# A fused attention and two-MLP kernel on one core: values in pairs, loads spread over the steps, and the last groups' scaling on ScalarE

## The chip, the core and the metric

The kernel runs on one core of a Trainium2 chip, as one program. The metric is the device time of one execution in microseconds. Three executions of the kernel before took 1492.85, 1494.42 and 1499.25 us; their median is 1494.42 us.

## What is computed

Talking-heads attention over 4 batches, 12 heads, 448 positions and head size 64, followed by two MLPs. All operands are float32.

```python
scores = scale * np.matmul(q, k.transpose(0, 1, 3, 2))
scores = np.einsum('bhij,hg->bgij', scores, w_pre)
scores = scores - np.max(scores, axis=-1, keepdims=True)
attn = np.exp(scores)
attn = attn / (np.sum(attn, axis=-1, keepdims=True) + 1e-09)
attn = np.einsum('bhij,hg->bgij', attn, w_post)
return np.matmul(attn, v).astype(np.float32)
...
gate = 1.0 / (1.0 + np.exp(-(x @ w_gate)))
val = x @ w_val
return (gate * val @ w_out).astype(np.float32)
...
h = np.maximum(x @ w_in, 0.0)
return (h * h @ w_out).astype(np.float32)
```

## The kernel before

The program issues every instruction by hand in one order (`tc.manual_schedule`), and each engine runs its own share of that order strictly in sequence. So the order of the work is decided in Python, in the function `attention` and in the generator `mlp`, which `whole` advances a piece at a time whenever `attention` yields.

**Units.** A batch's 448 rows are cut into four row tiles (110, 110, 110 and 118 rows, the last padded to 120), and a tile into groups of 10 rows (`GI`); there are 180 groups (`NG`) in all. A group lies in memory with 10 rows times 12 heads on 120 partitions, so that mixing over heads is one matmul with a block matrix. Two tiles make a chunk (8 chunks).

**Functions, by line of the profile.** `scores(n, p)` (L176) computes two heads' q times k for a whole tile, copies the two results out of PSUM, one on ScalarE (L189) and one on VectorE (L187), into `e`, and stores them with DMAs (L198) into the group layout `g`. `split(s)` makes a rounded part `gh` on ScalarE (L212) and the rest `gl` on GpSimd (L213). `premix(s)` mixes the heads on TensorE into `ps_m` (L222; three matmuls, of which the trace shows two as `gh` and one as `gl`). `maximum(s)` is on VectorE (L230), `exponent(s)` on ScalarE with the row sums (L238), `normal(s)` on VectorE (add L244, reciprocal L247) and then on GpSimd, which scales the post-mixing matrix by the reciprocal sums into `wn` (L249). `postmix(s)` multiplies with `wn` (L264, eight matmul records), and `mixed` copies the result into the chunk's `ap` on VectorE (L276). `values(c, h)` multiplies a head pair's `ap` with v (L293, sixteen records); `valued` copies it on ScalarE (L308) and stores it to `xs` (L309). `k_load` is at L148, `q_load` at L156, `v_load` at L283; k has 10 buffers (`KB`) of which 6 (`NP`) serve a batch, v has 4, and a chunk needs six v loads.

**Steps.** The main loop takes one step `s` for each group: premix of group s, what is pending from the step before (copies of postmix and values, v loads), maximum of s, exponent of s-1, normal of s-2, split of s+2, and then further TensorE work until an estimate `left_over` of the step's time is used up: scores of a later tile if they are ready, and from the list `back` either postmixes of groups up to s-3 (`LAG`) or, once a chunk's postmixes are all issued, its six `values`. Values may not stand in the step of the chunk's last postmix. The estimates are those of L24:

```python
MW, PW, VW, SW, STEP = 0.62, 0.82, 1.66, 1.04, 2.41
```

So one values, or two postmixes, or one postmix and one scores fill a step. The scores of a tile are ready from two steps before the tile before it begins, all six at once; the k load that replaces a used k is issued with the scores that use it, and a v load in the step after the values that free its buffer.

**The MLP's share.** In the last 112 steps (`EARLY`) the loop also yields to `mlp`: one piece for every three steps that have passed, but only in a step in which no postmix was issued; after the last scores, one piece a step. The first 28 pieces load and split the first `x` (L582, L598, L599) and prepare the first weights, in the stages `w_load` (L473), `w_bias` (ScalarE, L483), `w_high` (VectorE, L489 and L492), `w_low` (VectorE, L505 and L512), `w_sum` (GpSimd, L523), `w_round` (ScalarE, L529) and `w_rest` (GpSimd, L537). The MLPs' matmuls are at L669; the first of them are issued between the values of the last chunk, if their operands' pieces have been issued by then.

Of the kernel before, what the change touches and what calls it, by code (L numbers as in the profile page):

```python
# [11 lines left out]
ALU = mybir.AluOpType  # L12
# [7 lines left out]
HV = 2  # L20
LAG = 3
LA = 5
NA = 9
MW, PW, VW, SW, STEP = 0.62, 0.82, 1.66, 1.04, 2.41  # L24
KB = 10
# [29 lines left out]
def attention(tc, q, k, v, w_pre, w_post, xs, B, H, S, D):  # L55
# [10 lines left out]
    nc = tc.nc  # L66
    JT = S // JP
    NP = H // 2
# [12 lines left out]
    NG = len(groups)  # L81
# [6 lines left out]
    with ExitStack() as ctx, ExitStack() as mid, ExitStack() as left:  # L88
# [18 lines left out]
        wq = one.tile([KM, H, GI], F32, name="wq")  # L107
# [42 lines left out]
        def q_load(n, p0=0, p1=NP):  # L150
            if p0 == 0:
                q_t[n] = p2.tile([P, NP, IM], F32, tag="q", name="q")
            n0, isz = sum(full[:n]) * H * D, full[n]
            n1 = n0 + isz * H * D
            x = q[n0:n1].rearrange("(d p i) -> d p i", d=P, p=NP)
            nc.sync.dma_start(out=q_t[n][:, p0:p1, :isz], in_=x[:, p0:p1])  # L156
# [4 lines left out]
        def scores(n, p):  # L161

            b, i0, rows = tiles[n]
            isz = full[n]
            if p == 0:
                g_t[n] = pg.tile([KM, GT, S], F32, tag="g", name="g")
            kt = k_t.pop((b, p)) if i0 + rows == S else k_t[b, p]
            ps = [
                ps_b.tile([P, S], F32, tag="b", name="ps_s")
                if n == 0 and p % 2  # L170
                else ps_q.tile([P, S], F32, tag="q", name="ps_s")
                for _ in range(2)
            ]
            for o in range(2):
                r = slice(o * D, (o + 1) * D)
                nc.tensor.matmul(  # L176
                    ps[o][:isz], lhsT=q_t[n][r, p, :isz], rhs=kt[r], start=True, stop=True
                )
            if n == 0 and p >= 3:
                e = [pa.tile([IM, S], F32, tag="a", name="e0") for _ in range(2)]  # L180
            else:
                t = p4.tile([IM, 2, S], F32, tag="e", name="e")
                e = [t[:, o] for o in range(2)]
            to = g_t[n].rearrange("(r h) g j -> h r g j", h=H)
            for o in range(2):
                if o:
                    nc.vector.tensor_copy(e[o][:isz], ps[o][:isz])  # L187
                else:
                    nc.scalar.copy(e[o][:isz], ps[o][:isz])  # L189
                e0 = 0  # L190
                for m, (g0, g1) in enumerate(blocks(b, i0, i0 + rows)):
                    e1 = e0 + (g1 - g0) * GI
                    move = (to[2 * p + o, :, g0:g1], e[o][e0:e1])
                    if m:
                        second.append(move)
                    else:
                        queue = nc.scalar if n == 0 and o and p in (1, 3, 4, 5) else nc.sync
                        queue.dma_start(out=move[0], in_=move[1])  # L198
                    e0 = e1
# [16 lines left out]
        def premix(s):  # L216
            n, r0, rows = groups[s][:3]
            kk = rows * H
            ps = ps_m.tile([P, S], F32, tag="m", name="ps_m")
            hi, lo = parts.pop(s)  # L220
            for m, (w, x) in enumerate(((0, hi), (1, hi), (0, lo))):
                nc.tensor.matmul(  # L222
                    ps[:kk], lhsT=wp[w][:kk, :kk], rhs=x, start=m == 0, stop=m == 2
                )
            a_t[s] = ps

        def maximum(s):
            kk, ps = groups[s][2] * H, a_t[s]
            nm = pa.tile([KM, 1], F32, tag="nm", name="nm")
            nc.vector.tensor_reduce(out=nm[:kk], in_=ps[:kk], op=ALU.max, axis=AX.X, negate=True)  # L230
            a_t[s] = [ps, nm]

        def exponent(s):
            kk = groups[s][2] * H
            ps, nm = a_t[s]
            a = pa.tile([P, S], F32, tag="a", name="a")
            sm = pa.tile([KM, 1], F32, tag="sm", name="sm")
            nc.scalar.activation(a[:kk], ps[:kk], AF.Exp, bias=nm[:kk], accum_out=sm[:kk])  # L238
            a_t[s] = [a, sm]

        def normal(s):
            kk = groups[s][2] * H
            sm = a_t[s][1]
            nc.vector.tensor_scalar(  # L244
                out=sm[:kk], in0=sm[:kk], scalar1=1e-9, scalar2=None, op0=ALU.add
            )
            nc.vector.reciprocal(out=sm[:kk], in_=sm[:kk])  # L247
            wn = pa.tile([KM, H, GI], F32, tag="wn", name="wn")
            nc.gpsimd.tensor_scalar(  # L249
                out=wn[:kk], in0=wq[:kk], scalar1=sm[:kk], scalar2=None, op0=ALU.mult  # L250
            )
            a_t[s] = [a_t[s][0], wn]

        ap, pending = {}, []
# [58 lines left out]
        starts = [next(s for s in range(NG) if groups[s][0] == n) for n in range(NT)] + [NG]  # L313

        k_order = iter([(b, p) for b in range(B) for p in range(NP)])
        v_order = iter([(c, hv) for c in range(len(chunks)) for hv in range(H // HV)])

        def load_next(load, order):
            x = next(order, None)
            if x is not None:  # L320
                load(*x)


        front = []
        for n in range(1, NT):
            front += [(max(starts[n - 1] - 2, 0), starts[n] - LA, n, p) for p in range(NP)]
        def due(s):

            return any(z - 1 - i <= s for i, (_, z, _, _) in enumerate(front[:NP]))

        back = []
        for c, ch in enumerate(chunks):
            back += [(postmix, PW, s) for s in range(ch[3], ch[4])]
            back += [(values, VW, c, h) for h in range(0, H, 2)]
        bpos, closed, posted, behind = 0, False, {}, 0

        def next_scores():
            _, _, n, h = front.pop(0)
            scores(n, h)
            if tiles[n][1] + tiles[n][2] == S:  # L340
                load_next(k_load, k_order)
            if h == 0 and n + 1 < NT:
                q_load(n + 1)

        def flush():
            now, pending[:] = list(pending), []
            for f, *x in now:
                f(*x)
# [14 lines left out]
        for s in range(NG + 30):  # L363
            if s < NG:
                premix(s)
            flush()
            if s < NG:
                maximum(s)
            if s in (4, 5, 6, 7):
                load_next(v_load, v_order)  # L370
            if 8 <= s < 8 + KB - NP:
                load_next(k_load, k_order)
            if 1 <= s <= NG:
                exponent(s - 1)
            if 2 <= s < NG + 2:
                normal(s - 2)
            if s + 2 < NG:
                split(s + 2)
            left_over = STEP - MW
            ready = front and front[0][0] <= s  # L380
            if ready and due(s):
                next_scores()
                ready, left_over = False, left_over - SW
            while bpos < len(back) and (left_over > 0.5 or s >= NG):
                f, cost, *x = back[bpos]
                if f is postmix:
                    if x[0] > s - LAG:
                        break
                    posted[groups[x[0]][3]] = s
                elif posted[x[0]] == s:  # L390
                    if s < NG:
                        break
                    flush()
                elif posted[x[0]] == s - 1 and ready:
                    next_scores()
                    ready = False
                if len(pending) > 3:
                    flush()
                f(*x)
                if f is values and (x[1] + 2) % HV == 0:  # L400
                    pending.append((load_next, v_load, v_order))
                bpos += 1
                left_over -= cost
                if f is postmix and x[0] == NG - 1:
                    flush()
                    mid.close()
                if s >= NG:
                    yield 3 if bpos == len(back) or back[bpos][0] is values else 2
            if ready and left_over > 0.4:
                next_scores()  # L410
            if not front and not closed:
                left.close()
                closed = True
            if NG - EARLY <= s < NG:
                behind += 1
                if closed:
                    yield 2
                elif behind >= 3 and s not in posted.values():
                    behind -= 3
                    yield 1  # L420
# [406 lines left out]
```

## Time and profile before

| | |
|---|---|
| median of three executions | 1494.42 us |
| the profiled execution's own time | 1494.55 us |
| its span | 1492.8 us |
| TensorE matmul busy | 1464.9 us (98%) |
| VectorE, ScalarE, GpSimd busy | 808.3, 579.8, 709.6 us (54, 39, 48%) |
| DMA of the queues, mean | 124 GB/s |
| granted TensorE clock, mean of the span | 0.995 |

The span runs from the first to the last instruction; the execution's own time lies 1.75 us over it. A busy share is an average over stages that differ: the attention fills the first third, the MLPs the rest. Idle time of an engine counts only where another waits for it, so the stages are read one by one, by the order of TensorE and by what ended its idle times.

### The profile page before, as it was taken

Reading aid. Unit: us, or ns where it says so; the run is one execution under the profiler, and the core shown is the slowest. Engines: PE = TensorE matmul, PEld = TensorE weight load, DVE = VectorE, ACT = ScalarE, POOL = GpSimd, SP = SyncE. Lnnn points to the kernel's source line nnn. Section 1 sums busy time; section 2 is a strip of 40 time slices with the busy share of each in tenths; the row PEclk is TensorE's granted clock in tenths of the full one; section 3 lists DMA queues with packets and bytes.
Section 4 is the critical chain, followed back from the end, with each engine's and each line's share of the span. In section 5 each row is a group of like instructions: output and inputs, shape, how many; then the busy total and the mean of one; then the engine's idle time right before and its main releaser. Section 6 shows DMA issues by size and latency. Waiting matters only on the chain.

```text
span 1492.8 us, 21984 instructions
## 1 busy us (share of the span) xinstructions
PE 1464.9 (98%) x8028; PEld 1242.1 (83%) x8028; DVE 808.3 (54%) x1367; ACT 579.8 (39%) x1192; POOL 709.6 (48%) x583
## 2 busy tenths in 40 slices
PE   7989999999998999999999999999999999999999
PEld 3666766776676899999999999999999999999998
DVE  4757757668777487778889989901111101332000
ACT  4555555666654333332334443312222112333111
POOL 3756666766778355554545555522222222222221
PEclk9999999999999999999999999999999999999999
DMA  6554464564542354444444446531111121122221
GB/s 183 150 155 149 126 183 131 164 195 127 171 145 80 125 193 165 163 159 161 157 159 162 167 153 228 188 99 53 53 56 51 54 64 43 54 58 62 81 72 35
DMA packets 87688, 185.67 MB, mean 124 GB/s; under 512 B 17852, under 2 KB 54812, under 8 KB 87580
## 3 DMA queue, kind: packets, MB, share of 16 engines
q1 hardware_dynamic: 87220, 183.73, 38.8%
q8 instruction: 63, 1.03, 0.3%
q10 hardware_dynamic: 360, 0.54, 0.1%
q14 instruction: 45, 0.37, 0.1%
HBM read 107.78 MB, written 37.75 MB: 97 GB/s over the span
## 4 chain that ended last, share of the span: by engine, by line
PE 92%; DMA 4%; POOL 2%; issue 1%; DVE 1%; ACT 0%; SPq 0%; POOLq 0%; ACTq 0%; DVEq 0%
PE ps L669 67%; PE ps_p L264 8%; PE ps_m L222 7%; PE ps_s L176 5%; PE ps_v L293 5%; DMA g<-e 2%; DMA k<-in_k 1%; POOL gl L213 1%; DMA vraw<-in_v 1%; POOL wn L249 1%; DMA q<-in_q 0%; DVE ap L276 0%; ACT e L189 0%; POOL wl L537 0%; DVE nm L230 0%
## 5 line engine op out<-in xcount | busy, mean ns | idle before, releaser
L537 POOL TENSOR_TENSOR wl<-w,wh 128x768 fp32r<-128x768 f32 (+1 forms) x140 | 257.8, 1843 | 550.9 <-ACT wh L529 542.6
L669 PE MATMUL ps<-xh,wh 128*128 128x448 f32 x960 | 351.1, 366 | 0.0
L669 PE MATMUL ps<-xh,wl 128*128 128x448 f32 x960 | 350.7, 365 | 0.0
L669 PE MATMUL ps<-xl,wh 128*128 128x448 f32 x960 | 350.6, 365 | 0.0
L669 PE MATMUL ps<-hl,wh 128*128 128x448 f32 x672 | 246.8, 367 | 0.0
L669 PE MATMUL ps<-hh,wl 128*128 128x448 f32 x672 | 246.8, 367 | 0.0
L669 PE MATMUL ps<-hh,wh 128*128 128x448 f32 x672 | 246.7, 367 | 0.0
L213 POOL TENSOR_TENSOR gl<-g,gh 120x448 fp32r<-120x448 f32 x180 | 209.3, 1163 | 21.7 <-DMA q<-in_q 15.9
L264 PEld LDWEIGHTS ps_p<-wn,a 120*112 120x112 f32 (+1 forms) x1440 | 163.7, 177 | 43.8 <-issue 21.3
L669 PEld LDWEIGHTS ps<-xh,wh 128*128 128x128 f32 x960 | 180.3, 188 | 15.5 <-issue 1.0
L669 PEld LDWEIGHTS ps<-xh,wl 128*128 128x128 f32 x960 | 180.3, 188 | 14.5 <-POOL wl L537 0.2
L669 PEld LDWEIGHTS ps<-xl,wh 128*128 128x128 f32 x960 | 180.3, 188 | 14.2
L264 PE MATMUL ps_p<-wn,a 120*112 120x120 f32 (+1 forms) x1440 | 176.2, 270 | 6.9 <-POOL wn L249 6.7
L249 POOL TENSOR_SCALAR wn<-wq,sm 120x120 f32<-120x120 f32 x180 | 107.2, 595 | 132.8 <-DVE sm L247 99.1
L523 POOL TENSOR_TENSOR w<-w,w_f 128x768 f32<-128x768 f32 (+1 forms) x70 | 135.5, 1936 | 58.6 <-DVE w_f L512 58.6
L230 DVE TENSOR_REDUCE nm<-ps_m 120x1 f32<-120x448 f32 x180 | 111.9, 622 | 64.6 <-PE ps_m L222 64.2
L687 DVE TENSOR_TENSOR ps<-ps,sg 128x448 f32<-128x448 f32 x48 | 30.4, 632 | 197.8 <-PE ps L669 197.8
L669 PEld LDWEIGHTS ps<-hl,wh 128*128 128x128 f32 x672 | 126.1, 188 | 11.6
L669 PEld LDWEIGHTS ps<-hh,wh 128*128 128x128 f32 x672 | 126.1, 188 | 11.6
L669 PEld LDWEIGHTS ps<-hh,wl 128*128 128x128 f32 x672 | 126.1, 188 | 11.6
L238 ACT ACTIVATE a<-ps_m,nm 120x448 f32<-120x448 f32 x180 | 115.0, 639 | 47.9 <-DVE nm L230 46.5
L276 DVE COPY ap<-ps_p 112x480 f32<-112x480 f32 x180 | 117.0, 653 | 26.7 <-PE ps_p L264 26.7
(45 smaller groups left out, 1688.6 us busy)
## 6 DMA issues: line engine op xcount, KB each, us to landing
g<-e SPq DMA_DIRECT2D x132, 192.5 KB
ws<-w SPq DMA_DIRECT2D x58, 384.0 KB
w<-ws SPq DMA_DIRECT2D x58, 384.0 KB
w_raw<-in_wo SPq DMA_DIRECT2D x18, 768.0 KB
w_raw<-in_wi SPq DMA_DIRECT2D x16, 768.0 KB
vraw<-in_v SPq DMA_DIRECT2D x48, 224.0 KB
g<-e SPq DMA_DIRECT2D x48, 210.0 KB
w_raw<-in_wg SPq DMA_DIRECT2D x12, 768.0 KB
```

The source lines that it names most:

```text
L176: nc.tensor.matmul(ps[o][:isz], lhsT=q_t[n][r, p, :isz], rhs=kt[r], start=True, stop=True)
L213: nc.gpsimd.tensor_tensor(out=lo[:kk], in0=x, in1=hi[:kk].bitcast(F32), op=ALU.subtract)
L222: nc.tensor.matmul(ps[:kk], lhsT=wp[w][:kk, :kk], rhs=x, start=m == 0, stop=m == 2)
L230: nc.vector.tensor_reduce(out=nm[:kk], in_=ps[:kk], op=ALU.max, axis=AX.X, negate=True)
L238: nc.scalar.activation(a[:kk], ps[:kk], AF.Exp, bias=nm[:kk], accum_out=sm[:kk])
L249: nc.gpsimd.tensor_scalar(out=wn[:kk], in0=wq[:kk], scalar1=sm[:kk], scalar2=None, op0=ALU.mult)
L264: nc.tensor.matmul(ps[:JP, jt], lhsT=a[:kk, jt * JP : (jt + 1) * JP], rhs=wn[:kk].rearrange("p g i -> p (g i)"), start=True, stop=True,)
L276: nc.vector.tensor_copy(ap[c][:, :, :, g0 - i0 : g0 - i0 + rows], ps[:JP, :, :, :rows])
L293: nc.tensor.matmul(ps[o * D : (o + 1) * D, :w], lhsT=vraw[c, (h + o) // HV][:, (h + o) % HV, jt, :], rhs=ap[c][:, jt, h + o, :w], start=jt ...
L523: nc.gpsimd.tensor_tensor(out=x[:, s], in0=x[:, s], in1=fs.pop(n)[:, s], op=ALU.add)
L537: nc.gpsimd.tensor_tensor(out=lo[:, s], in0=w32.pop(n)[:, s], in1=h[:, s].bitcast(F32), op=ALU.subtract)
L669: nc.tensor.matmul(ps, lhsT=a, rhs=x, start=first and n == 0, stop=last and n == total - 1)
```

## The change

In the step loop a second `values` is issued right behind the first in the same step, whatever `left_over` says (`made % 2`). Scores of a tile become ready one after the other over the steps, not all at once. The k loads are counted as freed and issued one in every fourth step; of a chunk's v loads, the two that the same chunk still needs are issued as before, and the four for the next chunk one in every odd step. For the last 14 groups ScalarE makes `wn`, not GpSimd.

```diff
             wn = pa.tile([KM, H, GI], F32, tag="wn", name="wn")
-            nc.gpsimd.tensor_scalar(
-                out=wn[:kk], in0=wq[:kk], scalar1=sm[:kk], scalar2=None, op0=ALU.mult
-            )
+            if s < NG - 14:
+                nc.gpsimd.tensor_scalar(
+                    out=wn[:kk], in0=wq[:kk], scalar1=sm[:kk], scalar2=None, op0=ALU.mult
+                )
+            else:
+                nc.scalar.mul(wn[:kk], wq[:kk], sm[:kk])
...
         for n in range(1, NT):
-            front += [(max(starts[n - 1] - 2, 0), starts[n] - LA, n, p) for p in range(NP)]
+            a, z = max(starts[n - 1] - 2, 0), starts[n] - LA
+            front += [(a + p * (z - a) // NP, z, n, p) for p in range(NP)]
...
+        freed = [KB - NP, 0]
...
             if tiles[n][1] + tiles[n][2] == S:
-                load_next(k_load, k_order)
+                freed[0] += 1
...
-            if 8 <= s < 8 + KB - NP:
+            if s >= 8 and s % 4 == 0 and freed[0]:
                 load_next(k_load, k_order)
+                freed[0] -= 1
+            if s % 2 and freed[1]:
+                load_next(v_load, v_order)
+                freed[1] -= 1
...
-            while bpos < len(back) and (left_over > 0.5 or s >= NG):
+            made = 0
+            while bpos < len(back) and (left_over > 0.5 or s >= NG or made % 2):
...
                 f(*x)
+                made += f is values
                 if f is values and (x[1] + 2) % HV == 0:
-                    pending.append((load_next, v_load, v_order))
+                    if x[1] + 2 + 4 * HV <= H:
+                        pending.append((load_next, v_load, v_order))
+                    else:
+                        freed[1] += 1
```

How the order on the engines moves, at three places. First TensorE where the first chunk's values end, before (a values of a head pair reads here as `ps_v ... x8`, a premix as three `ps_m`, a postmix as `ps_p ... x4`):

```order
L293 MATMUL ps_v<-ap,vraw 64x220 x8
L222 MATMUL ps_m<-gh,wp_125 120x448
L222 MATMUL ps_m<-gh,wp_126 120x448
L222 MATMUL ps_m<-gl,wp_125 120x448
L264 MATMUL ps_p<-wn,a 112x120 x8
```

and now, with the chunk's last two pairs and a scores (`ps_s`) between them:

```order
L296 MATMUL ps_v<-ap,vraw 64x220 x16
L222 MATMUL ps_m<-gh,wp_125 120x448
L222 MATMUL ps_m<-gh,wp_126 120x448
L222 MATMUL ps_m<-gl,wp_125 120x448
L176 MATMUL ps_s<-k,q 120x448 x2
L296 MATMUL ps_v<-ap,vraw 64x220 x16
```

Two values stand behind one premix where one stood.

Second TensorE some steps later, now; the stretch has a step with a postmix and a scores, a step with a postmix alone, and again one with both:

```order
L267 MATMUL ps_p<-wn,a 112x120 x4
L176 MATMUL ps_s<-k,q 110x448 x2
L222 MATMUL ps_m<-gh,wp_125 120x448
L222 MATMUL ps_m<-gh,wp_126 120x448
L222 MATMUL ps_m<-gl,wp_125 120x448
L267 MATMUL ps_p<-wn,a 112x120 x4
L222 MATMUL ps_m<-gh,wp_125 120x448
L222 MATMUL ps_m<-gh,wp_126 120x448
L222 MATMUL ps_m<-gl,wp_125 120x448
L267 MATMUL ps_p<-wn,a 112x120 x4
L176 MATMUL ps_s<-k,q 110x448 x2
```

Before, the steps around here hold two postmixes, or a scores and a postmix, and none holds a postmix alone.

Third VectorE at steps 168 and 169, before (`nm` is the maximum, `sm` the two operations of normal, `ap` the copy of a postmix):

```order
L230 TENSOR_REDUCE nm<-ps_m 120x1
L244 TENSOR_SCALAR sm<-sm 120x1
L247 RECIPROCAL sm<-sm 120x1
L276 COPY ap<-ps_p 112x48x10 x2
L230 TENSOR_REDUCE nm<-ps_m 120x1
```

and now:

```order
L230 TENSOR_REDUCE nm<-ps_m 120x1
L244 TENSOR_SCALAR sm<-sm 120x1
L247 RECIPROCAL sm<-sm 120x1
L520 TENSOR_SCALAR w_t<-w_5561 128x768
L527 SCALAR_TENSOR_TENSOR w_f<-w_raw,w_t 128x768
L279 COPY ap<-ps_p 112x48x10
L230 TENSOR_REDUCE nm<-ps_m 120x1
```

Two operations of the MLP's weights (`w_t`, `w_f`) have come between the sums and the copy; six such pairs now stand at steps 165, 168, 170, 173, 174 and 176, where they stood at 139, 142, 160, 163, 164 and 166.

## Rows read from the trace of the kernel before

**Rows 1.** Busy time by window, two stages; columns us, then each engine.

```profile
79.58:442.29 362.71, 356.69 (x2470) 248.79 (x2468) 254.28 (x646) 214.63 (x547) 248.03 (x287) 1.00 0.51 153
442.29:481.21 38.92, 32.55 (x228) 26.82 (x227) 30.56 (x73) 20.63 (x51) 34.97 (x37) 0.96 0.29 91
```

**Rows 2.** Timeline, TensorE: a step with one values, a step with two postmixes.

```profile
206.75 0.67 PE L222 MATMUL ps_m<-gh,wp 120*120 120x448 f32 x2
...
207.54 1.71 PE L293 MATMUL ps_v<-ap,vraw 112*64 112x220 f32 x16
209.18 0.67 PE L222 MATMUL ps_m<-gh,wp 120*120 120x448 f32 x2
...
218.43 0.64 PE L222 MATMUL ps_m<-gh,wp 120*120 120x448 f32 x2
...
219.11 1.80 PE L264 MATMUL ps_p<-wn,a 120*112 120x120 f32 x16
220.68 0.65 PE L222 MATMUL ps_m<-gh,wp 120*120 120x448 f32 x2
```

**Rows 3.** Timeline, TensorE: premixes of four steps with one postmix each.

```profile
35.72 0.65 PE L222 MATMUL ps_m<-gh,wp 120*120 120x448 f32 x2
...
37.16 0.65 PE L222 MATMUL ps_m<-gh,wp 120*120 120x448 f32 x2
...
39.07 0.65 PE L222 MATMUL ps_m<-gh,wp 120*120 120x448 f32 x2
...
40.74 0.65 PE L222 MATMUL ps_m<-gh,wp 120*120 120x448 f32 x2
```

**Rows 4.** Timeline, all engines: a step with a postmix and a scores, after another.

```profile
74.46 0.66 PE L222 MATMUL ps_m<-gh,wp 120*120 120x448 f32 x2
...
74.60 0.62 DVE L187 COPY e<-ps_s 120x448 f32<-120x448 f32 x1 [0.58 <-PE ps_s L176]
...
75.16 0.98 PE L264 MATMUL ps_p<-wn,a 120*112 120x120 f32 x8
...
75.71 0.61 DVE L230 TENSOR_REDUCE nm<-ps_m 120x1 f32<-120x448 f32 x1
...
76.68 0.59 POOL L249 TENSOR_SCALAR wn<-wq,sm 120x120 f32<-120x120 f32 x1 [0.86 <-DVE sm L247]
...
77.02 0.66 PE L222 MATMUL ps_m<-gh,wp 120*120 120x448 f32 x2
```

**Rows 5.** Timeline: TensorE after idle times, and one issue of a v load on SP.

```profile
82.00 1.12 PE L176 MATMUL ps_s<-k,q 64*120 64x448 f32 x4 [1.55 <-ACT e L189]
...
95.29 3.19 PE L293 MATMUL ps_v<-ap,vraw 112*64 112x220 f32 x16 [2.42 <-DMA vraw<-in_v]
...
205.26 0.34 SPq L283 DMA_DIRECT2D vraw<-in_v  x1
...
212.09 1.71 PE L293 MATMUL ps_v<-ap,vraw 112*64 112x220 f32 x16 [2.04 <-DMA vraw<-in_v]
```

**Rows 6.** Busy time by window, two steps of the end stretch; granted clock third from last.

```profile
469.50:474.30 4.80, 4.72 (x22) 3.66 (x22) 3.48 (x7) 1.32 (x4) 4.80 (x6) 0.64 0.01 2
```

**Rows 7.** Groups by line, VectorE, 70 to 480 us: preparation for the MLP.

```profile
L599 DVE TENSOR_TENSOR xl<-xr,xh 128x448 fp32r<-128x448 f32 x6 | 6.1, 1016 | 1.7 <-ACT xh L598 1.7
L492 DVE SCALAR_TENSOR_TENSOR w<-w_f,w_t 128x768 uint32<-128x768 uint32 x3 | 3.8, 1260 | 0.1
L512 DVE SCALAR_TENSOR_TENSOR w_f<-w_raw,w_t 128x768 f32<-128x768 uint32 x3 | 3.0, 987 | 0.2
L505 DVE TENSOR_SCALAR w_t<-w 128x768 uint32<-128x768 uint32 x3 | 2.7, 914 | 0.0
L489 DVE TENSOR_SCALAR w_t<-w_f 128x768 uint32<-128x768 uint32 x3 | 1.7, 573 | 0.0
```

**Rows 8.** Groups by line and shape, ScalarE, whole span.

```profile
L308 ACT COPY xo<-ps_v 128x220 f32<-128x220 f32 x24 | 8.2, 342 | 23.0 <-PE ps_v L293 22.8
```

**Rows 9.** Timeline, VectorE: the copy of the last postmix.

```profile
481.49 0.56 DVE L276 COPY ap<-ps_p 112x384 f32<-112x384 f32 x1 [0.99 <-PE ps_p L264]
```

## The prediction

> **What bounds the kernel now.** I first cut the span into its stages (busy time by window). The reader should see [rows 1] that between 79.58 and 442.29 us TensorE is busy 356.69 of 362.71 us, so there its own order sets the time, and that the end of the attention, 442.29 to 481.21, is different: TensorE 32.55 of 38.92, GpSimd 34.97, VectorE 30.56, ScalarE 20.63. What follows 481.21 is the two MLPs, back to back on TensorE, with the last chunk's six `values` among them; the change doesn't alter those instructions.
>
> Second, the timeline of TensorE, read from the start of one premix to the start of the next: the length of a step. A step with one `values` (I write V) takes 209.18 - 206.75 = 2.43 us, of which the premix 0.79 and V 1.64; a step with two postmixes (pp) 2.25, with 0.68 from premix to postmix [rows 2]. A step with one postmix alone (p) takes 1.44 when nothing holds it, then 1.91 for the next and 1.67 for the one after [rows 3]: a run of p steps isn't bound by TensorE. A step with a postmix and a scores (ps) takes 77.02 - 74.46 = 2.56 [rows 4]. So far hardly any p step lies between 79.58 and 442.29; spare time goes into V, pp and ps.
>
> Third, the idle times of TensorE there: a score's PSUM copy waiting for stores, 1.55; values waiting for v, 2.42 and, within the 3.19 us that the V takes instead of 1.71, 1.48 more; and 2.04 [rows 5]. Together 7.5 us in 363.
>
> **The change part by part.**
>
> *Order on TensorE.* By the order, a chunk's six V now stand as three pairs in three successive steps, two of them with scores, and not in six steps. The three premixes that were among them now stand beside postmixes: pp steps fall from six to three a chunk, and six or seven p steps appear, since scores are spread out too. From step 25 to the step where the last chunk's stretch begins (163 now, 166 before) there are 18 pp, 60 ps, 39 p and 21 pairs of V (counted in the order), where there were 36 pp, 63 ps and 42 V.
> - One pair: two V steps were 4.86. Now 0.79 + 2 x 1.64 = 4.07, plus the moved premix, which turns a pp into two p: 2 x 1.44 - 2.25 = 0.63. So 4.70, a gain of 0.16, and for 21 pairs **-3.4 us**.
> - Three premixes move past the boundary into the end stretch: 3 x 0.68 = **-2.0**, given back there.
> - *The new wait.* The postmix of a p or ps step needs the scaled weights `wn` of three groups back. The chain that makes them is in rows 4: after a ps step VectorE first copies its scores (74.60), then the postmix's result, then takes the maximum (75.71), then the sums; GpSimd scales from 76.68 to 77.27. If the step at 74.46 had no scores, its successor would begin at 74.46 + 1.44 = 75.90 and want its postmix 0.70 later (75.16 - 74.46), at 76.60. It gets `wn` at 77.27: 0.67 us late. Queued behind that postmix on TensorE are this step's scores and the next premix, so all is late. This is the price that I take for each of the 15 p steps that stand alone: 10.1. For each of the six runs of four I take 0.67 and twice 1.67 - 1.44 = 0.23: 6 x 1.13 = 6.8. Sum **+16.8**. The lower end for a single p is 0.23 (the steady run of rows 3), 0.47 (1.91 - 1.44) lies between; 0 would ask for no dependence at all. I take 0.67 because it is worked out at a ps step, which is where the new p steps stand.
> - Before step 25 one ps becomes a p (-1.1) and two p stand alone (2 x 0.67): **+0.2**.
>
> *Loads.* k loads go from one a scores to one every fourth step, v loads from behind each V to every odd step, except the two that the running chunk still needs. They issue on SP, whose queue they no longer fill in the steps of the scores' stores. The three stalls of rows 5 were all next to such loads; I count all 7.5 as gone: **-7.5** (lower end: none gone, 0). What is late next is the fifth v load of a chunk: it issues at the premix behind the first pair and is used at the third, 0.79 + 2 x 1.64 + 0.79 + (2.56 - 1.44) = 6.0 us later. In rows 5 a load issued at 205.26 let its V start at 212.09, 6.83 later. With that queue it would come 0.8 late in each of seven chunks; with the spread queue I take 0 and keep 0.8 x 7 = 6 as the upper end.
>
> *The end stretch.* The MLP's first weights are prepared in steps without a postmix, one piece each. Six V steps a chunk were such steps, now three are: half the places are gone. By VectorE's order five of the first six pieces of preparation stood before the end stretch (in V steps, on an idle VectorE); now all six stand in steps 165 to 176. Their price [rows 7]: 3 x (0.573 + 1.260) + 3 x (0.914 + 0.987) = 11.2 us, of which one piece of 1.9 lay there already: +9.3. Two of three `xl` subtractions leave (2 x 1.02, rows 7): -2.0. Three more groups' maximum, taken as 0.61 [rows 4], and sums (0.3 an estimate from the 76.68 - 75.71 - 0.61 = 0.36 between them): +2.7. VectorE's load becomes 30.6 + 9.3 - 2.0 + 2.7 = 40.6 us. In return 14 scalings of 0.59 [rows 4] leave GpSimd: 8.3 off its 35.0 [rows 1], so it stops being the bound. On ScalarE they are at most 0.34 each, the time of a copy of 220 elements where these have 120 [rows 8]: 14 x 0.34 = 4.8 on top of 20.6, covered by its idle 18 us; if that cover went, 4.8 would show. The bound therefore moves from GpSimd at 35.0 to VectorE at 40.6. Before, 38.9 - 35.0 = 3.9 us were waiting beside the bound; I keep them: 44.5 against 38.9, **+5.6**. Ends: 40.6 with no waiting (+1.7); and 44.5 + 4.8.
>
> *Behind the last postmix* no MLP matmuls are ready in time (their preparation is late), so three V follow at once; the first needs the last postmix's copy, which ends at 481.49 + 0.56 = 482.05 where matmuls used to go on at 481.21 [rows 9]: **+0.8**.
>
> Sum: -3.4 - 2.0 + 16.8 + 0.2 - 7.5 + 5.6 + 0.8 = +10.5. The profiled execution took 1494.55 us (span 1492.8); it is 0.13 over the median of the runs, 1494.42. I predict **1505 us**, slower by 0.7%. A measurement of this kernel can tell about 0.5%, 7.5 us, from no change: below 1486.9 is faster, above 1501.9 slower.
>
> **The rivals.**
> 1. *The waits are small: about the same.* If `wn` comes 0.23 late for each p step (15 x 0.23 + 6 x 0.69 = 7.6 for 16.8), the sum is +1.3: about 1496. For it: rows 3 show 1.67 in the steady run. Against it: that run has no scores to copy on VectorE.
> 2. *No waits and the loads' gain: faster.* Without the 16.8 and with the end stretch at VectorE's bare 40.6, the sum is -3.4 - 2.0 + 0.2 - 7.5 + 1.7 + 0.8 = -10.2: about 1484. It decides at the place where the successor of a single p asks for `wn`: if VectorE reaches the maximum 0.67 us earlier than in rows 4. For it: VectorE and GpSimd idle in the pairs and could get ahead there. Against it: the maximum can't come before its premix, and the score copy stands before it.
> 3. *The clock falls in the end stretch: slower still.* The granted clock was 0.64 on average from 469.50 to 474.30, a part of it at the lower of 1.2 and 2.4 GHz; these 4.80 us are two p steps, 2.40 each instead of 1.67 [rows 3, 6]. If the 13 p steps of the end all ran so, 13 x 0.73 = 9.5 comes on top: about 1514. Against it: over the whole end stretch the mean was 0.96 [rows 1], so the clock fell for a small part of it only, though TensorE was busy for just 32.55 of 38.92 us. The Trainium skill (TensorE: Matmul & The Clock Gate, Part 1) has it that the slow clock is the default and that activity releases it, so that a stretch with more idling would pay. By that rule the end would be at the 9.5 rather than at nothing; the trace agrees that the clock falls there, and shows it for a tenth of the stretch.
> 4. *Fifth and sixth v loads late:* +6, about 1511, as worked out above.
> That the change doesn't do what it says is partly seen in the order: the pairs stand in three successive steps, not in every second one. This is in the sum.
>
> **How the numbers follow.** Forecast 0.40, rivals 3 and 4 together 0.12: slower 0.52. Rival 1: 0.34, the same. Rival 2: 0.14, faster. The range leaves out most of rival 2 and the far end of rival 3: 1487 to 1514. The forecast's own range is 1502 to 1510.
>
> **What would show it.** Steps of a pair near 4.1 us; the step behind a single p near 3.2 with an idle time on TensorE put down to `wn`; no idle time over 1 us for `e`, k or v; an end stretch of 44 us with VectorE its busiest engine. I am wrong if the step behind a p takes 2.56, or if VectorE idles through the end stretch.

## The result, and the profile after

The changed kernel takes 1511.76 us, the median of four executions (1509.87 to 1513.11), against 1493.68 for the kernel before measured beside it: a ratio of 1.011 (95% interval 1.009 to 1.0131): slower, by 18 us in the medians and by 16 by the ratio. The profiled execution took 1513.11 us, with a span of 1511.4 (before: 1494.55 and 1492.8).

First the busy time by window of the changed kernel: steps 25 to 162, the end stretch up to the first values behind the last postmix, and a piece of that stretch. Columns: us, TensorE, its weight loads, VectorE, ScalarE, GpSimd, granted clock, DMA share, GB/s.

```profile
78.85:446.79 367.94, 356.16 (x2464) 251.93 (x2463) 237.29 (x628) 211.51 (x536) 237.15 (x280) 1.00 0.47 142
446.79:497.64 50.85, 39.62 (x238) 32.75 (x236) 41.25 (x91) 29.25 (x75) 29.88 (x26) 0.87 0.35 105
455.58:463.48 7.90, 7.33 (x34) 6.39 (x34) 5.97 (x15) 4.40 (x12) 4.83 (x5) 0.59 0.31 78
```

Against [rows 1] the first stretch is 5.2 us longer, with the same TensorE work in it (356.2 for 356.7), and the end stretch 11.9 longer (50.85 for 38.92). VectorE is its busiest engine, GpSimd no longer is. Step 25 begins 0.7 earlier. What follows 497.64 takes 1013.8 instead of 1011.6: the first six values there run in 11.8 us of TensorE time, not 10.1. -0.7 + 5.2 + 11.9 + 2.1 = 18.5, the difference of the spans but for rounding (18.6).

Next the timeline of a step with one postmix (p) and its successor with postmix and scores (ps), the answer to [rows 4]:

```profile
104.37 0.68 PE L222 MATMUL ps_m<-gh,wp 120*120 120x448 f32 x2
...
105.09 0.98 PE L267 MATMUL ps_p<-wn,a 120*112 120x120 f32 x8
...
105.84 0.65 PE L222 MATMUL ps_m<-gh,wp 120*120 120x448 f32 x2
...
106.59 0.58 POOL L250 TENSOR_SCALAR wn<-wq,sm 120x120 f32<-120x120 f32 x1 [0.85 <-DVE sm L247]
...
107.23 1.07 PE L267 MATMUL ps_p<-wn,a 120*112 120x120 f32 x8 [0.54 <-POOL wn L250]
...
108.23 1.01 PE L176 MATMUL ps_s<-k,q 64*110 64x448 f32 x4
...
109.17 0.66 PE L222 MATMUL ps_m<-gh,wp 120*120 120x448 f32 x2
```

The p step takes 1.47, its successor 3.33. A ps that nothing holds takes 2.56 [rows 4], so the price of a single p is 0.77 to 0.80 in all 15 places between steps 25 and 162. TensorE idles for 0.54 of it until `wn` is there; the rest doesn't show as idle time. Two steps with a pair of values, without scores (from 438.00) and with them (from 433.11):

```profile
433.11 0.67 PE L222 MATMUL ps_m<-gh,wp 120*120 120x448 f32 x2
...
434.87 3.19 PE L296 MATMUL ps_v<-ap,vraw 112*64 112x220 f32 x32
438.00 0.66 PE L222 MATMUL ps_m<-gh,wp 120*120 120x448 f32 x2
...
441.92 0.67 PE L222 MATMUL ps_m<-gh,wp 120*120 120x448 f32 x2
```

They take 3.92 and 4.89. And what TensorE waited for from step 25 to the end stretch, in the groups by line (the last column is idle time and its releaser):

```profile
L267 PE MATMUL ps_p<-wn,a 120*112 120x120 f32 (+1 forms) x1080 | 133.3, 269 | 11.7 <-POOL wn L250 11.7
...
L176 PE MATMUL ps_s<-k,q 64*110 64x448 f32 (+1 forms) x296 | 74.9, 582 | 0.0
L296 PE MATMUL ps_v<-ap,vraw 112*64 112x220 f32 (+1 forms) x666 | 67.5, 355 | 0.1
```

The stalls of [rows 5] at scores and values are gone; waiting for `wn` has come in their place.

Last the end stretch, three places in its timeline:

```profile
454.02 0.89 ACT L498 ACTIVATE w_f<-w_raw 128x768 f32<-128x768 f32 x1 [4.49 <-DMA w_raw<-in_wg]
454.81 0.62 ACT L238 ACTIVATE a<-ps_m,nm 120x448 f32<-120x448 f32 x1
...
455.58 0.67 PE L222 MATMUL ps_m<-gh,wp 120*120 120x448 f32 x2 [1.79 <-ACT a L238]
...
468.49 1.77 DVE L507 SCALAR_TENSOR_TENSOR w<-w_f,w_t 128x768 uint32<-128x768 uint32 x1
...
471.65 0.39 ACT L254 ACTIVATE wn<-wq,sm 120x120 f32<-120x120 f32 x1 [2.84 <-DVE sm L247]
...
472.10 1.07 PE L267 MATMUL ps_p<-wn,a 120*112 120x120 f32 x8 [2.11 <-ACT wn L254]
...
484.36 2.14 POOL L538 TENSOR_TENSOR w<-w,w_f 128x768 f32<-128x768 f32 x1
...
484.90 2.40 DVE L527 SCALAR_TENSOR_TENSOR w_f<-w_raw,w_t 128x768 f32<-128x768 uint32 x1
...
486.45 1.85 POOL L213 TENSOR_TENSOR gl<-g,gh 120x448 fp32r<-120x448 f32 x1
...
488.35 0.46 PE L222 MATMUL ps_m<-gl,wp 120*120 120x448 f32 x1 [2.21 <-POOL gl L213]
```

In each a piece of the MLP's preparation stands ahead of the attention's own chain on an engine that works in order. At 454.02 ScalarE has waited 4.49 us for a weight load, with the exponent queued behind it, and TensorE's premix waits for that. At 468.49 VectorE makes a weight's high part while the postmix copy, the maximum and the sums queue; ScalarE idles for 2.84 until the sums are there and it can make `wn`, and TensorE 2.11 until `wn` is. At 484.90 `w_f` takes 2.40 us beside GpSimd's `w`, and GpSimd takes up `gl` only behind `w`.

### The profile page after: what moved, and what is told of

It reads as the page before. It is cut to its first block, busy times and chain, and to the rows that moved or that the text cites. A ratio compares the mean times of both kernels' runs of the same rounds, so it can differ in the third digit from the quotient of the medians.

```text
span 1511.4 us, 22057 instructions
## 1 busy us (share of the span) xinstructions
PE 1471.2 (97%) x8028; PEld 1251.3 (83%) x8028; DVE 814.0 (54%) x1367; ACT 585.8 (39%) x1206; POOL 699.6 (46%) x569
## 4 chain that ended last, share of the span: by engine, by line
PE 66%; DVE 1%; ACT 0%; DMA 0%; issue 0%; POOL 0%; ACTq 0%; POOLq 0%
PE ps L684 65%; PE ps_v L296 1%; DMA w_raw<-in_wv 0%; DVE w_f L527 0%; ACT a L238 0%; POOL wl L552 0%; DVE ap L279 0%; ACT wn L254 0%; DVE w_t L520 0%; PE ps_p L267 0%; ACT xh L613 0%; ACT wh L544 0%; DVE xl L614 0%; ACT gh L212 0%; ACT o L716 0%
## 5 line engine op out<-in xcount | busy, mean ns | idle before, releaser
L267 PEld LDWEIGHTS ps_p<-wn,a 120*112 120x112 f32 (+1 forms) x1440 | 169.3, 179 | 46.3 <-POOL wn L250 32.8
L267 PE MATMUL ps_p<-wn,a 120*112 120x120 f32 (+1 forms) x1440 | 182.2, 273 | 19.0 <-POOL wn L250 14.1
L250 POOL TENSOR_SCALAR wn<-wq,sm 120x120 f32<-120x120 f32 x166 | 97.0, 584 | 149.5 <-DVE sm L247 134.1
L222 PE MATMUL ps_m<-gh,wp 120*120 120x448 f32 x360 | 120.9, 417 | 8.4 <-ACT gh L212 5.4
L544 ACT CAST wh<-w 128x768 fp32r<-128x768 f32 (+1 forms) x140 | 113.4, 814 | 36.8 <-POOL w L538 36.8
```

What stands on the lines that cost most here:

```text
L222: nc.tensor.matmul(ps[:kk], lhsT=wp[w][:kk, :kk], rhs=x, start=m == 0, stop=m == 2)
L250: nc.gpsimd.tensor_scalar(out=wn[:kk], in0=wq[:kk], scalar1=sm[:kk], scalar2=None, op0=ALU.mult)
L267: nc.tensor.matmul(ps[:JP, jt], lhsT=a[:kk, jt * JP : (jt + 1) * JP], rhs=wn[:kk].rearrange("p g i -> p (g i)"), start=True, stop=True,)
L544: nc.scalar.copy(h[:, s], w32[n][:, s])
```

## The experiments

The theory that I started from (W): the waits for `wn` behind single p steps, and preparation pushed into the end stretch, where VectorE's work bounds. The rivals: (A) the scaling on ScalarE stretches the end; (B) GpSimd and VectorE are too slow as a whole; (L) spreading loads and scores brings nothing.

**1. The changed kernel with all scaling on GpSimd.**

```diff
-            if s < NG - 14:
+            if s < NG:
```

> The changed kernel (1511.8 us) with one part undone: GpSimd scales wn for all groups. Theory W (the loss is waits for wn behind single-postmix steps, and MLP preparation pushed into the end stretch, where VectorE is the bound): the end stretch, 50.0 us from the last chunk's first double postmix to its last postmix, stays within 3 us of that, since VectorE keeps its 40.7 us of work; total 1509 to 1515. Rival A (scaling on ScalarE in its strict order is what stretches the end): the end stretch falls by 5 us or more; total 1506 or less.

Measured: 1512.64 us, ratio to before 1.0125 (1.011 to 1.014). No gain: in the changed kernel the scaling's engine doesn't matter. The end stretch takes 50.95 for 50.85, with GpSimd now about as busy as VectorE:

```profile
446.72:497.67 50.95, 39.13 (x238) 32.99 (x236) 39.94 (x92) 25.71 (x61) 40.57 (x40) 0.87 0.37 115
```

**2. The changed kernel with up to two preparation pieces in a step without a postmix.**

```diff
-                elif behind >= 3 and s not in posted.values():
-                    behind -= 3
-                    yield 1
+                else:
+                    for _ in range(2):
+                        if behind >= 3 and s not in posted.values():
+                            behind -= 3
+                            yield 1
```

> The changed kernel with up to two pieces of MLP preparation, not one, in a step without a postmix, so that as many pieces as before the change are issued ahead of the end stretch. Theory W: VectorE's load in the end stretch falls from 40.7 to about 31 us, the end stretch from 50 to 38 to 42 us, and the MLP's first matmuls stand between the last values again; total 1498 to 1503. Rival A (ScalarE's scaling): the end stretch keeps 46 us or more; total 1508 or more.

Measured: 1514.33, ratio 1.0142 (1.0123 to 1.0161). This contradicts W. VectorE's load in the end stretch fell from 41.25 to 35.15, and the stretch by 2.2 only; the main stretch grew by 4.9, 3.3 of it idle time before values that wait for v (the preparation's loads now come together with the v loads; that this is why is not shown). VectorE's load was not the bound:

```profile
452.08:500.75 48.67, 39.08 (x238) 32.92 (x236) 35.15 (x84) 28.03 (x74) 32.45 (x27) 0.86 0.37 112
```

**3. The changed kernel with postmixes four groups back.**

```diff
-LAG = 3
+LAG = 4
```

> The changed kernel with postmixes one more step behind (LAG 4 for 3), so that wn has a whole further step to be made. Theory W: the step behind a single-postmix step falls from 3.35 to 2.56 us (15 times 0.79 us, and twice before step 25), runs of four keep about 1.67 a step because GpSimd and VectorE need that; total 12 to 17 us less, 1495 to 1500. Rival B (these steps are long because GpSimd or VectorE as a whole are too slow, not because of when wn is asked for): the idle time moves by one step and stays; total 1507 or more.

Measured: 1499.41, ratio 1.0026 (1.0009 to 1.0042), so 12.5 us less than the changed kernel. The timeline has the p and its successor from 108.80:

```profile
108.80 0.68 PE L222 MATMUL ps_m<-gh,wp 120*120 120x448 f32 x2
...
110.27 0.65 PE L222 MATMUL ps_m<-gh,wp 120*120 120x448 f32 x2
...
112.81 0.67 PE L222 MATMUL ps_m<-gh,wp 120*120 120x448 f32 x2
```

The ps behind a single p takes 2.54: its price was the dependence on `wn`, and this is shown. In the runs of four it isn't. Their third p now takes 2.13 to 2.23 in five of the six, and a run still costs 1.14 to 1.56 us, 1.2 on average, where it cost 1.49:

```profile
118.13 1.14 POOL L213 TENSOR_TENSOR gl<-g,gh 120x448 fp32r<-120x448 f32 x1
118.24 0.65 PE L222 MATMUL ps_m<-gh,wp 120*120 120x448 f32 x2
119.24 0.59 POOL L250 TENSOR_SCALAR wn<-wq,sm 120x120 f32<-120x120 f32 x1
119.33 0.47 PE L222 MATMUL ps_m<-gl,wp 120*120 120x448 f32 x1 [0.43 <-POOL gl L213]
```

TensorE waits for `gl` instead, and GpSimd goes from one `wn` and `gl` to the next without a gap, 1.67 us for each group, which is also the length of the further p steps. So in a run GpSimd's pace sets the time, as rival B had it. From the first pair of values to the last chunk's first pp the kernel gained 10.0 us (357.93 for 367.94): some 7 stay in the runs, and TensorE idled 2.0 for v and 0.9 for `e` again.

**4. The changed kernel without pairs.**

```diff
-            while bpos < len(back) and (left_over > 0.5 or s >= NG or made % 2):
+            while bpos < len(back) and (left_over > 0.5 or s >= NG):
```

> The changed kernel without the pairs (one values a step again, the spread loads and scores and ScalarE's scaling kept). Theory W: no single-postmix steps, preparation back in the values' steps, and the loads' stalls (7.5 us of the kernel before) still gone; total 1482 to 1489, under the kernel before. Rival L (spreading loads and scores brings nothing or costs): 1493 or more.

Measured: 1494.34, ratio 1.0002 (0.9988 to 1.0017), above what W said and the time that L gave. The last chunk's stretch began 3.8 us earlier than before, but the end stretch took 43.30. Preparation was where it had been before; so something else lengthens the end. New theory (S): with the preparation early, the scaling on ScalarE does cost.

**5. The kernel before with spread loads and scores alone** (number 4 with `if s < NG:` for the scaling).

> The kernel before with the spread loads and scores alone: values one by one, all scaling on GpSimd. Theory S (new): the ScalarE scaling by itself makes the end stretch longer, because ScalarE takes its work in order and wn then stands between the sums and the split of the next group. Without it the end stretch is back at 38.9 us, while the 3.8 us that the spread loads gave up to step 166 stay: 1489 to 1491. Rival N (ScalarE is not the cause; the spread loads or scores make the end longer themselves): as with the scaling on ScalarE, 1493 to 1495, end stretch 43.

Measured: 1490.05, ratio 0.9968 (0.9955 to 0.9981). As S, and against L: the end stretch is back.

```profile
436.92:475.84 38.92, 32.56 (x229) 27.23 (x227) 30.25 (x73) 20.63 (x51) 34.95 (x37) 0.96 0.31 96
```

**6. The kernel before with the last 14 groups' scaling on ScalarE**, the first hunk of the change alone.

> The kernel before with one edit, the scaling of the last 14 groups on ScalarE. Theory S: end stretch 43 us against 38.9, time 1497 to 1499. Rival N: end stretch 39 or less (GpSimd relieved), time 1492 to 1494.

Measured: 1498.78, ratio 1.0033 (1.0016 to 1.0049). As S. The window of the end stretch, and its largest wait in the timeline:

```profile
441.97:485.39 43.42, 33.99 (x228) 29.28 (x227) 32.15 (x73) 24.82 (x65) 27.87 (x23) 0.92 0.35 108
```

```profile
475.01 2.98 DVE L602 TENSOR_TENSOR xl<-xr,xh 128x448 fp32r<-128x448 f32 x1 [1.39 <-ACT xh L601]
...
475.68 1.82 POOL L526 TENSOR_TENSOR w<-w,w_f 128x768 f32<-128x768 f32 x1
...
479.38 0.39 ACT L254 ACTIVATE wn<-wq,sm 120x120 f32<-120x120 f32 x1 [3.78 <-DVE sm L247]
...
479.82 1.07 PE L267 MATMUL ps_p<-wn,a 120*112 120x120 f32 x8 [3.33 <-ACT wn L254]
```

GpSimd, 7 us less busy, takes up its `w` earlier and beside VectorE's `xl`, which lasts 2.98 us; before, no `xl` in that stretch lasted longer than 1.55. The maximum and the sums wait behind `xl`, `wn` for the sums, TensorE for `wn`. This place has most of the loss: of the 4.5 us by which the stretch is longer, 3.7 come behind the premix of step 179, at 475.65. Number 4 has the same there (`xl` at 471.43 lasts 2.97). That ScalarE makes the end longer is shown; that it does so by way of this collision is read from these places, and no run kept the two operations apart.

**7. The changed kernel with two pieces (number 2) and all scaling on GpSimd.**

> The changed kernel with up to two pieces of preparation in a step without a postmix and all scaling on GpSimd. Theory S (with the waits behind single postmix steps as before): the two causes that lengthen the end are both gone, end stretch 39 to 42 us, time 1503 to 1508; the waits remain. Rival D (the end is bound by what the moved premixes, postmixes and the clock do, whoever scales and wherever the preparation stands): end stretch 48 to 50, time 1512 to 1515.

Measured: 1512.34, ratio 1.0119 (1.0093 to 1.0146): as rival D, not S. Of the preparation's pairs on VectorE two stand in the end stretch here, where the changed kernel has six and the kernel before one, and the scaling is back on GpSimd. With the two causes nearly undone the end stretch still takes 47.25, now with GpSimd the busiest, and the main stretch is 4 us longer for v loads that are late again (3.8 idle, 3.7 of it for v).

```profile
450.17:497.42 47.25, 38.42 (x237) 32.55 (x236) 34.34 (x84) 24.16 (x60) 39.52 (x42) 0.86 0.32 97
```

**8. The same with LAG = 4.**

> The changed kernel with LAG 4, up to two pieces in a step without a postmix, all scaling on GpSimd. If the waits for wn (about 12 us) and the end stretch's two causes are the whole loss: 1489 to 1494, as fast as the kernel before or a little faster, with the loads' gain left over. If the end doesn't shorten (rival D): 1499 to 1502.

Measured: 1495.56, ratio 1.0002 (0.9985 to 1.0019), between the two expectations: the waits for `wn` are gone, but GpSimd's `gl` (2.5 us of TensorE's idle time before the end stretch) and v (2.9) hold TensorE again, and the end stretch is 45.4, so the pairs bring nothing over the kernel before.

That left two theories of the end: (T) each of its steps costs some 2.5 us, and pairs at the last boundary put three more steps into it; (P) the late preparation.

**9. Number 1 with pairs at every boundary but the last.** VectorE's order of the preparation stays that of the changed kernel.

```diff
-            while bpos < len(back) and (left_over > 0.5 or s >= NG or made % 2):
+            while bpos < len(back) and (left_over > 0.5 or s >= NG or made % 2 and s < 155):
```

> The changed kernel with all scaling on GpSimd and with pairs at every boundary but the last (steps 160 to 165 hold one values each, as before). VectorE's order of the MLP's preparation stays as in the changed kernel (steps 165 to 176). Theory T (each step of the end stretch costs about 2.5 us whatever TensorE has in it, 32.85 us for 13 steps before; pairs at the last boundary push three more steps into it): end stretch 39 to 41 us from the first pp on, time 1502 to 1505. Theory P (the preparation that VectorE must do in the end stretch makes it long): still 46 to 48 us, time 1509 to 1512.

Measured: 1510.01, ratio 1.0098 (1.0067 to 1.013): the time that P gave. The three steps are worth some 4 us against number 1 (1.0125), not 8 to 10. The step in front of the end stretch took 3.2 us too long, by the same wait for a weight load as at 454.02 above; the end stretch itself was 43.3, shorter than P said and longer than T did.

**10. The kernel before with preparation in even steps only.** The order on TensorE is as before up to the last postmix, the preparation on VectorE at the changed kernel's steps.

```diff
-                elif behind >= 3 and s not in posted.values():
+                elif behind >= 3 and s % 2 == 0 and s not in posted.values():
```

> The kernel before with one edit: preparation pieces only in even steps, so that VectorE's six pieces stand at steps 165 to 176, exactly as in the changed kernel; the steps' order on TensorE is as before. Theory P: end stretch 44 to 48 us against 38.9, time 1500 to 1504. Theory T: end stretch 39 to 40, time 1494 to 1497 (up to 1 us for the values that now follow the last postmix at once).

Measured: 1506.8, ratio 1.0077 (1.0048 to 1.0107): slower, as P said and by more than P said; the end stretch alone takes 43.3, a little less than it said. No pair, no spread load, no scaling on ScalarE is in this kernel. Its step 165 and end stretch as one window, then places of its timeline:

```profile
442.51:490.86 48.35, 35.92 (x247) 30.42 (x246) 37.62 (x86) 23.63 (x56) 37.84 (x38) 0.93 0.34 109
```

```profile
445.74 0.89 ACT L483 ACTIVATE w_f<-w_raw 128x768 f32<-128x768 f32 x1 [4.12 <-DMA w_raw<-in_wg]
...
447.54 0.67 PE L222 MATMUL ps_m<-gh,wp 120*120 120x448 f32 x2 [2.52 <-ACT a L238]
...
475.60 2.12 POOL L523 TENSOR_TENSOR w<-w,w_f 128x768 f32<-128x768 f32 x1
...
476.15 2.39 DVE L512 SCALAR_TENSOR_TENSOR w_f<-w_raw,w_t 128x768 f32<-128x768 uint32 x1
...
479.04 1.07 PE L264 MATMUL ps_p<-wn,a 120*112 120x120 f32 x8 [2.77 <-POOL wn L249]
```

Two of the three places shown of the changed kernel, in the same order. The window took 41.36 before: 7.0 longer, 6.1 of it idle time of TensorE. The part behind it grew by 1.9, as in the changed kernel; another 2.7 of this execution are values that waited for v in the main stretch. The kernel of number 6, which has no edit there, has the like (a step with a values takes 7.25 us at 204.83, 7.63 at 207.75 here, 4.55 before), so the edit isn't needed to explain them.

So the late preparation alone lengthens the end, and it is not all. Side by side: late preparation without pairs at the last boundary, +7.0 (number 10) and, by the same window, +7.6 (number 9: 48.92 for 41.36); pairs at the last boundary, which put three more groups into the end stretch, with the preparation nearly back, +8.3 (number 7: 47.25 for 38.92); both, +12.0 (number 1: 50.95). Each by itself costs 7 to 8 us, as P and T had it, and together they cost less than their sum. That is why undoing one of them gained so little in numbers 2, 7 and 9.

**11. Number 5 with a tile's scores ready all at once**, so the spread loads alone.

```diff
-            front += [(a + p * (z - a) // NP, z, n, p) for p in range(NP)]
+            front += [(a, z, n, p) for p in range(NP)]
```

> The kernel before with the spread k and v loads alone: scores six at once, values one by one, scaling on GpSimd. If the loads alone take the stalls (7.5 us) away, and the spread scores only brought single p steps (0.8 us for each of the five there): 1486 to 1488. If the spread scores did part of it: 1490 to 1493.

Measured: 1487.64, ratio 0.9947 (0.9924 to 0.9969). The loads alone take the stalls away (idle times of lines 176 and 296 from step 25 on, 1.6 and 4.5 before):

```profile
L176 PE MATMUL ps_s<-k,q 64*110 64x448 f32 (+1 forms) x294 | 74.5, 581 | 0.3 <-ACT e L189 0.3
L296 PE MATMUL ps_v<-ap,vraw 112*64 112x220 f32 (+1 forms) x672 | 72.7, 358 | 0.0
```

**12. Number 5 with LAG 4 up to step 139.**

```diff
-                    if x[0] > s - LAG:
+                    if x[0] > s - (4 if s < 140 else LAG):
```

> Spread loads and spread scores, values one by one, scaling on GpSimd, and postmixes four groups back until step 139, three from then on. If a single p step's price is the wait for wn and nothing else, the five of them (0.8 us each) cost nothing now: 3 to 4 us under the run with spread loads and scores alone, 1486 to 1487. If it is the step's own work on VectorE, no change: 1490.

Measured: 1485.84, ratio 0.9934 (0.9911 to 0.9957): the fastest kernel here, 10 us under the kernel before, and 4 under number 5, as the first expectation had it (the two intervals just touch, at 0.9957 and 0.9955). No wait for `wn` is left from step 25 to the end stretch. It and number 11 can't be told apart by their intervals.

## Why the prediction was right, and where not

The sign and the range held (1505 forecast, 1487 to 1514; measured 1511.76), though the forecast's own range, 1502 to 1510, was missed by 1.8 us. The time lies where rival 4 (1511) had put it, but not for its reason: the end of the attention cost more than was priced, and that the whole stayed inside the range is in part luck. By its steps:

- *Pairs*, -3.4: -5.5. A pair without scores took 3.97 on average (3.92 to 4.04 in seven steps) where 4.07 was taken from twice the V of a lone values; 4.86 - 3.97 - 0.63 = 0.26 for each of 21. The 4.86 is of a chunk with 220 columns and the 3.97 of both kinds of chunk; 220 columns alone give 4.86 - 3.93 - 0.63 = 0.30.
- *Waits for `wn`*, +16.8: +20.8. Single p: 15 x 0.79 for 15 x 0.67; the place was right to the step, and 0.12 was missing from the size. Runs of four: 1.49 each for 1.13, because the second of the run also takes 2.24 rather than 2.11 and the ps behind the run 0.22 more. Number 3 shows the dependence on `wn` to be the cause for the single p, 11.9 of the 20.8; of the 8.9 in the runs of four it took away only some 1.5, and the rest is GpSimd's pace. Rivals 1 and 2 fell with these steps.
- *Before step 25*, +0.2: -0.7. No run shows what gave the rest.
- *Loads*, -7.5: right. Number 11 gives 1 - 0.9947 = 0.0053 of 1495.5, 7.9 us (4.6 to 11.4 by its interval). The fifth v load (rival 4) stalled nothing.
- The stretch as a whole: -5.5 - 2.0 + 20.8 - 7.5 = +5.8 by these terms, +5.2 in the windows; +3.9 was predicted.
- *End stretch and the values behind it*, +5.6 and +0.8: +11.9 with both. This is the term that was mis-sized. VectorE's load was right (41.25 for 40.6), and it became the busiest engine as said. The step that failed is "Before, 38.9 - 35.0 = 3.9 us were waiting beside the bound; I keep them": beside 41.25 there were 9.6. The moved preparation was priced as VectorE's time, but it is a chain over a weight load, ScalarE, VectorE and GpSimd, and in each of the places shown a late piece stands in front of the attention's own chain on one of them. Number 10 has the price of the move alone, 7.0 us in step 165 and the end stretch. The three more groups were priced as VectorE's time too, 2.7 us; number 7, with the preparation nearly back, has them at 8.3. So VectorE was no bound that its load could have told (number 2).
- *ScalarE's scaling*, "covered by its idle 18 us": in the changed kernel it is (number 1 for the change), in the kernel before it is not (number 6: +4.9). One scaling took 0.39 where at most 0.34 was taken. That the late preparation ended later than these waits did, and so hid them, is argued and not shown.
- *What follows the attention* was taken as unchanged; it is 2.1 longer, of which 1.7 the six values that ran partly at the lower clock (0.55 granted from 497.64 to 500.36).
- *The clock*, rival 3, was left out of the forecast and was partly right: the granted clock was 0.87 over the end stretch, 0.59 from 455.58 to 463.48, behind the wait for the weight load. The p step at 460.76 ran at 0.50, the lower level of 1.2 GHz, with TensorE busy throughout, and took 2.72. TensorE's own count of the 11.9 us is 7.1 more busy time (39.62 for 32.55), of which the three premixes are 2.0 and the rest, 5.1, matmuls that took longer, and 4.8 more idle time. In number 10 it is 0.9 busy and 6.1 idle, in number 7 5.9 busy (2.0 of it premixes again) and 2.5 idle. So the clock is little of what late preparation costs by itself, but in the changed kernel it can have cost up to 5 us, and in number 7 up to 4. What it alone cost isn't separated by any run, since it fell further in every kernel whose end had longer waits.

The sum of the parts, one at a time, goes: spread loads 0.9947, with spread scores 0.9968, with ScalarE's scaling 1.0002, with the pairs 1.011. Only the first part gains; the second step is inside the intervals. The pairs, the part that names the change, cost 16 us, net of what TensorE's order gains: the waits for `wn` and GpSimd's pace behind the p steps, three more groups in the end stretch, and the places for preparation that they take away.

## What to carry to other kernels

A cheaper order on the busiest engine changes which steps are short; look in each shortened step for the result that it now asks for sooner, and in a run of such steps for the engine that can't keep their pace. When background work moves, price it by its whole chain and by what queues behind it on every in-order engine, not by its busy time on one. And try the parts of a mixed change one at a time: here spreading the loads was worth 8 us, hidden under pairs that lost 16.

## What the runs showed of the hardware

VectorE and GpSimd hold each other up where the operands of both lie in SBUF, and one that begins with nothing ahead of it is not slowed. Two places of the kernel before, and one of the changed kernel, in the timeline:

```profile
443.40 1.83 POOL L523 TENSOR_TENSOR w<-w,w_f 128x768 f32<-128x768 f32 x1
...
443.99 1.65 DVE L505 TENSOR_SCALAR w_t<-w 128x768 uint32<-128x768 uint32 x1
...
445.75 0.96 DVE L512 SCALAR_TENSOR_TENSOR w_f<-w_raw,w_t 128x768 f32<-128x768 uint32 x1
446.06 1.64 POOL L213 TENSOR_TENSOR gl<-g,gh 120x448 fp32r<-120x448 f32 x1
```

```profile
454.94 0.56 DVE L504 TENSOR_SCALAR w_t<-w_f 128x768 uint32<-128x768 uint32 x1 [1.87 <-ACT w_f L498]
```

At 443.99 a `w_t` begun behind GpSimd's `w` took 1.65 (0.56 with GpSimd idle) and ended 0.41 behind it; at 445.75 `w_f` began first and took 0.96, and GpSimd's `gl` became 1.64 instead of 1.14. The same `w_f` took 2.40 above, begun behind a `w`, and `xl` took 2.98 in number 6, 0.62 where nothing held it. That `xl` began while a `gl` ran (474.58 to 475.72) and 0.67 before the `w` at 475.68, and still lasted until 0.49 behind the `w`, which took its usual 1.82; above, the waiting `w_f` went ahead of the next `gl`, which took 1.85. So one that waits can be passed over, and these rows don't tell when. Maxima and copies out of PSUM kept their 0.61 and 0.65 throughout. The Trainium skill (SBUF — State Buffer, the section "SBUF: two separate sides") has the pair of ports that the two engines share as an exclusive lock, which whoever starts first holds for its whole instruction, where VectorE's operation has two SBUF inputs and GpSimd's reads SBUF, or VectorE's runs in a two-port mode. These rows agree that one waits for the other's whole instruction; which of two goes next, after a wait, they leave open. So an edit that relieves GpSimd can lengthen VectorE's work, by moving GpSimd's next operation beside it, as in number 6.
